# Splitting the packed weights p'·w_in into float32r halves once a batch, straight from PSUM, in an attention-and-FFN kernel

## The chip, the core and the metric

The kernel runs on one core of a Trainium2 chip. A core has a matrix engine (TensorE, PE in the profile; its weight loads are PEld), a vector engine (VectorE, DVE), an activation engine (ScalarE, ACT), GpSimd (POOL), and SyncE (SP), whose queue issues the DMAs here. The metric is the device time of one execution in microseconds (us). Each engine works through its own queue of instructions in order and waits at the head of the queue for what an instruction needs.

## The reference

For 8 batches, 8 heads, 576 tokens and 64 numbers a head, 32 packed queries p first attend to k and v, and then every token's q attends to that packed result, which serves as key and value. The result, 4608 tokens of 512 numbers, passes a two-layer network with a leaky rectifier whose slope alpha is a number per hidden unit.

```python
def sm_attn(qq, kk, vv):
    s = scale * np.matmul(qq, kk.transpose(0, 1, 3, 2))
    s = s - np.max(s, axis=-1, keepdims=True)
    a = np.exp(s)
    a = a / (np.sum(a, axis=-1, keepdims=True) + 1e-09)
    return np.matmul(a, vv)
p_packed = sm_attn(p, k, v)
out = sm_attn(q, p_packed, p_packed)        # (8, 8, 576, 64)
x = out.transpose(0, 2, 1, 3).reshape(B * S, H * D)
h = x @ w_in                                # (4608, 2048)
g = np.maximum(h, 0.0) + alpha * np.minimum(h, 0.0)
return g @ w_out                            # (4608, 512)
```

## The kernel before, in words

Since the second attention multiplies weights a' (32 per head and token) by the packed result p', x·w_in equals a'·(p'·w_in). The kernel therefore never forms x. `attention(b)` makes p' (`p2[b]`) and then the normalised weights a' of a batch (`result[b]`). `packed_w(b, j)` makes p'·w_in for 512 hidden units at a time (j = 0 to 3) with 16 small matmuls (L343) into two PSUM banks, which ScalarE copies to SBUF (L348) as the tile `pw[b, j]`.

The network runs in steps. A step is a pair (k, f): token half k (288 tokens; batch k // 2) and a block f of 128 hidden units. `first(k, f)` multiplies pw by a' into a bank `ps_h` (two of them in turn); ScalarE makes the negated relu (`neg`, L398), VectorE applies alpha in place (L399), ScalarE rounds to float32r (`gh`, L405), and VectorE makes the rest (`gl`, L406). `second(k, f)`, two steps behind, adds gh·w_out high, gh·w_out low and gl·w_out high into four banks `acc` (L416 to L418). Such sums of three products with split operands stand for a float32 product.

For `first` there are two ways. Batches below `XF` = 2 multiply in plain float32: a' is one tile `a_f`, pw is float32, and a step has two matmuls (L384). Later batches split both: a' into `a_h` and `a_l`, made once a batch by ScalarE (L333) and GpSimd (L334), and pw into `pwh` and `pwl` by `split_pw` (L372 and L373 on VectorE), once for each token half and each pair of blocks f, 16 times a batch. A step then has six matmuls (L392 to L394). For batches from 2 on, two instructions of the second softmax (L309, L317) run on GpSimd, for batches 0 and 1 on VectorE.

Batch 0's attention runs alone at the start. After it, 256 steps run. The first 64 cover batches 0 and 1 in four sweeps, so that w_out can arrive in parts: k = 0 and 1 with f = 0 to 3 and then 4 to 7, k = 2 and 3 with f = 0 to 7 (steps 16 to 31), and then all four with f = 8 to 15 (batch 1 in steps 48 to 63). From step 64 on each batch takes 32 steps. In the first 64 steps the weights are also turned from float64 into float32 by ScalarE and VectorE (L101 to L137), after the table `pieces`.

Other work is spread over the steps by tables of step numbers: `attention(b)` is a generator, one stage a step, from step T + 2 with T = 32(b − 1), and `packed_w_steps(b)` reloads w_in from DRAM and calls `packed_w`, at T + 21, 23, 25, 27, 29. What such a step adds is issued behind that step's `first`, relu and alpha (`marks`). Within these bounds a scheduler sets the order of each engine's queue, so a change of one part can reorder the rest.

Of the kernel before, what the change touches and what calls it, by code (L numbers as in the profile page):

```python
# [25 lines left out]
def pack_attention_ffn_kernel(  # L26
# [38 lines left out]
    pwp = ctx.enter_context(tc.tile_pool(name="pwp", bufs=8))  # L65
    pwj = ctx.enter_context(tc.tile_pool(name="pwj", bufs=2))
# [151 lines left out]
    def attention(b):  # L218
# [120 lines left out]
    def packed_w(b, j):  # L339
# [6 lines left out]
        pw[b, j] = pwp.tile([P, 2, 512], F32, name="pw", tag="pw")  # L346
        for r in range(2):
            nc.scalar.copy(out=pw[b, j][:, r, :], in_=banks[r])  # L348
# [19 lines left out]
    def split_pw(k, h):  # L368
        src = pw[k // 2, h // 2][:, :, (h % 2) * 256 : (h % 2) * 256 + 256]
        th = pwj.tile([P, 2, 256], F32R, name="pwh", tag="pwh")  # L370
        tl = pwj.tile([P, 2, 256], F32R, name="pwl", tag="pwl")
        nc.vector.tensor_copy(out=th, in_=src)  # L372
        nc.vector.tensor_tensor(out=tl, in0=src, in1=fv(th), op=ALU.subtract)  # L373
        pj[k, h] = (th, tl)

    def first(k, f):
# [3 lines left out]
        if b < XF:  # L380
            th, a_f = pw[b, f // 4], result[b]
            fs = slice((f % 4) * P, (f % 4) * P + P)
            for i in range(2):
                mm = nc.tensor.matmul(x, th[:, i, fs], a_f[:, i, tok], start=(i == 0), stop=(i == 1))  # L384
        else:
            if (k, f // 2) not in pj:
                split_pw(k, f // 2)
            th, tl = pj[k, f // 2]
# [1 line left out]
            fs = slice((f % 2) * P, (f % 2) * P + P)  # L390
            for i in range(2):
                nc.tensor.matmul(x, th[:, i, fs], a_h[:, i, tok], start=(i == 0), stop=False)  # L392
                nc.tensor.matmul(x, th[:, i, fs], a_l[:, i, tok], start=False, stop=False)  # L393
                mm = nc.tensor.matmul(x, tl[:, i, fs], a_h[:, i, tok], start=False, stop=(i == 1))  # L394
# [142 lines left out]
```

## Time and profile before

| | |
|---|---|
| median of 3 runs | 764.77 us (764.04 to 765.14) |
| profiled execution | 764.46 us |
| its span, first to last instruction | 762.7 us |
| granted TensorE clock, mean | 0.986 |
| TensorE busy | 731.1 us (96%) |
| VectorE busy | 493.5 us (65%) |
| ScalarE busy | 344.9 us (45%) |
| GpSimd busy | 53.1 us (7%) |

A row of a group of instructions reads: line, engine, operation, what it writes `<-` what it reads, shape, count, then busy time and mean ns of one, then idle time of the engine ahead of them and who ended it. A row of the timeline reads: start, length (both us), engine, line, operation, and in brackets the idle time ahead of it with its releaser. Durations of neighbouring instructions of an engine overlap, so what one costs its engine is read from start to start. A float32 matmul of the program appears as more than one MATMUL in the profile. In a row of windows the length is followed by the busy time of PE, PEld, DVE, ACT and POOL, the granted clock, the DMA share and the GB/s.

### The profile page before, as it was taken

The numbers are of one execution on the slowest core, as the hardware profiler recorded it, in microseconds if no ns is written. First come the engines' busy times: TensorE is split into PE (matmuls) and PEld (weight loads), VectorE is DVE, ScalarE is ACT, GpSimd is POOL, SyncE is SP. The second block draws the span as 40 slices with busy tenths as digits, with TensorE's granted clock in tenths as the row PEclk, the third lists the DMA queues.
The fourth block names the chain that finished last, engine by engine and source line by source line (L and its number), as shares of the span: only waits on it lengthen the run. The fifth ranks groups of instructions, "written<-read, shape, count | busy, mean of one in ns | idle before, by whom it ended". The sixth has DMA issues, their size and how long they took to land.

```text
span 762.7 us, 15606 instructions
## 1 busy us (share of the span) xinstructions
PE 731.1 (96%) x6232; PEld 648.2 (85%) x6232; DVE 493.5 (65%) x1019; ACT 344.9 (45%) x795; POOL 53.1 (7%) x74
## 2 busy tenths in 40 slices
PE   4499999999999999999999999999999999999997
PEld 2277788788878999899989999799988999899997
DVE  4887898775545576565855667555765657556663
ACT  4466466663333434443444534444434534443332
POOL 0000000002100021000300012000210003000000
PEclk8699999999999999999999999999999999999999
DMA  8969144044262241422233231422324100200000
GB/s 295 384 226 348 63 166 166 1 137 141 87 197 87 67 126 71 182 86 75 94 113 111 97 119 39 166 88 87 111 78 166 63 2 32 111 33 1 32 1 32
DMA packets 51673, 85.44 MB, mean 112 GB/s; under 512 B 4496, under 2 KB 32144, under 8 KB 51600
## 3 DMA queue, kind: packets, MB, share of 16 engines
q1 hardware_dynamic: 51600, 84.44, 32.1%
q8 instruction: 49, 0.80, 0.4%
q14 instruction: 24, 0.20, 0.1%
HBM read 70.79 MB, written 13.63 MB: 111 GB/s over the span
## 4 chain that ended last, share of the span: by engine, by line
PE 87%; DVE 4%; DMA 4%; ACT 2%; issue 1%; SPq 1%; ACTq 0%; POOL 0%; DVEq 0%
PE acc L416 17%; PE acc L418 17%; PE acc L417 17%; PE ps_h L384 7%; PE ps_h L392 7%; PE ps_h L394 7%; PE ps_h L393 6%; PE ps_m L343 4%; PE ps_m L204 2%; DMA vraw<-in_v 1%; PE ps_m L281 1%; DMA wraw<-in_w_out 1%; PE ps_m L262 1%; DMA wraw<-in_w_in 1%; SPq L121 1%
## 5 line engine op out<-in xcount | busy, mean ns | idle before, releaser
L416 PE MATMUL acc<-gh,wo 128*128 128x288 f32 x1024 | 294.8, 302 | 5.7 <-ACT gh L405 4.5
L417 PE MATMUL acc<-gh,wo 128*128 128x288 f32 x1024 | 290.5, 296 | 0.7 <-DVE wo L137 0.7
L418 PE MATMUL acc<-gl,wo 128*128 128x288 f32 x1024 | 249.7, 306 | 0.0
L416 PEld LDWEIGHTS acc<-gh,wo 128*128 128x128 f32 x1024 | 191.6, 188 | 23.7 <-issue 12.2
L398 ACT ACTIVATE neg<-ps_h 128x288 f32<-128x288 f32 x256 | 105.6, 412 | 208.2 <-PE ps_h L394 155.8
L417 PEld LDWEIGHTS acc<-gh,wo 128*128 128x128 f32 x1024 | 192.5, 188 | 4.1 <-issue 1.7
L399 DVE SCALAR_TENSOR_TENSOR ps_h<-neg,nal,ps_h 128x288 f32<-128x288 f32 x256 | 131.7, 517 | 97.2 <-ACT neg L398 96.8
L418 PEld LDWEIGHTS acc<-gl,wo 128*128 128x128 f32 x1024 | 172.7, 188 | 22.8 <-issue 18.3
L405 ACT CAST gh<-ps_h 128x288 fp32r<-128x288 f32 x256 | 102.4, 400 | 151.2 <-DVE ps_h L399 147.5
L406 DVE TENSOR_TENSOR gl<-ps_h,gh 128x288 fp32r<-128x288 f32 x256 | 115.8, 453 | 77.7 <-ACT gh L405 77.1
L392 PE MATMUL ps_h<-a_h,pwh 128*128 128x288 f32 x384 | 114.6, 298 | 0.0
L394 PE MATMUL ps_h<-a_h,pwl 128*128 128x288 f32 x384 | 114.2, 297 | 0.0
L393 PE MATMUL ps_h<-a_l,pwh 128*128 128x288 f32 x384 | 113.1, 295 | 0.0
L384 PE MATMUL ps_h<-a_f,pw 128*128 128x288 f32 x256 | 75.6, 421 | 8.8 <-DVE z L314 6.7
L392 PEld LDWEIGHTS ps_h<-a_h,pwh 128*128 128x128 f32 x384 | 72.1, 188 | 2.8 <-DVE gl L406 2.3
L394 PEld LDWEIGHTS ps_h<-a_h,pwl 128*128 128x128 f32 x384 | 72.0, 188 | 2.8 <-issue 2.3
L393 PEld LDWEIGHTS ps_h<-a_l,pwh 128*128 128x128 f32 x384 | 72.1, 188 | 0.0
L373 DVE TENSOR_TENSOR pwl<-pw,pwh 128x512 fp32r<-128x512 f32 x96 | 66.8, 697 | 6.5
L372 DVE CAST pwh<-pw 128x512 fp32r<-128x512 f32 x96 | 40.6, 424 | 40.7 <-PE ps_h L393 40.1
L384 PEld LDWEIGHTS ps_h<-a_f,pw 128*128 128x128 f32 x256 | 46.3, 195 | 20.9 <-issue 9.1
L343 PE MATMUL ps_m<-w,p 64*32 64x512 f32 x512 | 38.7, 612 | 0.0
L348 ACT COPY pw<-ps_m 128x512 f32<-128x512 f32 x64 | 34.8, 596 | 2.4 <-PE ps_m L343 2.3
(73 smaller groups left out, 444.5 us busy)
## 6 DMA issues: line engine op xcount, KB each, us to landing
w<-w_whole SPq DMA_DIRECT2D x48, 512.0 KB, 4.0
outT<-ot SPq DMA_DIRECT2D x64, 144.0 KB, 1.9
wraw<-in_w_in SPq DMA_DIRECT2D x8, 1024.0 KB, 11.7
wraw<-in_w_out SPq DMA_DIRECT2D x8, 1024.0 KB, 6.3
xraw<-in_kT SPq DMA_DIRECT2D x28, 288.0 KB, 4.3
xraw<-in_qT SPq DMA_DIRECT2D x28, 288.0 KB, 3.6
vraw<-in_v SPq DMA_DIRECT2D x28, 256.0 KB, 3.5
w_whole<-w SPq DMA_DIRECT2D x8, 512.0 KB, 4.8
```

Source lines behind the costliest of these rows:

```text
L343: nc.tensor.matmul(banks[r][cs, :], p2[b][rs, cs], wi_t[j, pr][rs, :], start=True, stop=True)
L384: mm = nc.tensor.matmul(x, th[:, i, fs], a_f[:, i, tok], start=(i == 0), stop=(i == 1))
L392: nc.tensor.matmul(x, th[:, i, fs], a_h[:, i, tok], start=(i == 0), stop=False)
L393: nc.tensor.matmul(x, th[:, i, fs], a_l[:, i, tok], start=False, stop=False)
L394: mm = nc.tensor.matmul(x, tl[:, i, fs], a_h[:, i, tok], start=False, stop=(i == 1))
L398: nc.scalar.activation(out=neg, in_=x, func=AF.Relu, scale=-1.0),
L399: nc.vector.scalar_tensor_tensor(out=x, in0=neg, scalar=nal[:, f : f + 1], in1=x, op0=ALU.mult, op1=ALU.add),
L405: nc.scalar.copy(out=gh, in_=x)
L406: nc.vector.tensor_tensor(out=gl, in0=x, in1=fv(gh), op=ALU.subtract)
L416: nc.tensor.matmul(ps, wo_t[f][:, 0, os_], gh, start=begin, stop=False)
L417: nc.tensor.matmul(ps, wo_t[f][:, 1, os_], gh, start=False, stop=False)
L418: nc.tensor.matmul(ps, wo_t[f][:, 0, os_], gl, start=False, stop=end)
```

## The change

`XF` becomes 1, so that batch 1 takes the split products too; the constant `EARLY` = 2 keeps what `XF` set for the order of batch 1's loads. `split_pw` goes. For batches from `XF` on `packed_w` writes a tile of both halves: ScalarE's copy out of PSUM rounds to float32r (line 353 of the changed kernel), and VectorE subtracts that from the same PSUM bank (line 354). These tiles are twice as large, and their pool has five buffers in place of eight, with the pool of `split_pw` gone. The second softmax's two instructions run on GpSimd from batch 1 on. Attention starts a step later, and `packed_w` comes at T + 20, 23, 26, 29, with its first reload at T + 17. In the changed kernel L398, L399, L405, L406 are L392, L393, L399, L400, L416 to L418 are L410 to L412, and the split products are L386 to L388.

```diff
-    pwp = ctx.enter_context(tc.tile_pool(name="pwp", bufs=8))
-    pwj = ctx.enter_context(tc.tile_pool(name="pwj", bufs=2))
+    pwp = ctx.enter_context(tc.tile_pool(name="pwp", bufs=5))
...
-        if b < XF:
+        if b < EARLY:
             vs = load_v(b, ("wo2", "wo3") if b == 0 else None)
...
-            eng = nc.vector if b < 2 else nc.gpsimd
+            eng = nc.vector if b < 1 else nc.gpsimd
...
-        pw[b, j] = pwp.tile([P, 2, 512], F32, name="pw", tag="pw")
-        for r in range(2):
-            nc.scalar.copy(out=pw[b, j][:, r, :], in_=banks[r])
+        if b < XF:
+            pw[b, j] = pwp.tile([P, 2, 512], F32, name="pw", tag="pw")
+            for r in range(2):
+                nc.scalar.copy(out=pw[b, j][:, r, :], in_=banks[r])
+        else:
+            pw[b, j] = pwp.tile([P, 2, 2, 512], F32R, name="pw", tag="pw")
+            for r in range(2):
+                hi, lo = pw[b, j][:, 0, r, :], pw[b, j][:, 1, r, :]
+                nc.scalar.copy(out=hi, in_=banks[r])
+                nc.vector.tensor_tensor(out=lo, in0=banks[r], in1=fv(hi), op=ALU.subtract)
...
-    def split_pw(k, h):
-        src = pw[k // 2, h // 2][:, :, (h % 2) * 256 : (h % 2) * 256 + 256]
-        th = pwj.tile([P, 2, 256], F32R, name="pwh", tag="pwh")
-        tl = pwj.tile([P, 2, 256], F32R, name="pwl", tag="pwl")
-        nc.vector.tensor_copy(out=th, in_=src)
-        nc.vector.tensor_tensor(out=tl, in0=src, in1=fv(th), op=ALU.subtract)
-        pj[k, h] = (th, tl)
...
+        w, fs = pw[b, f // 4], slice((f % 4) * P, (f % 4) * P + P)
+        for i in range(2):
+            if b < XF:
+                mm = nc.tensor.matmul(
+                    x, w[:, i, fs], result[b][:, i, tok], start=(i == 0), stop=(i == 1)
+                )
+                continue
             a_h, a_l = result[b]
...
+            nc.tensor.matmul(x, w[:, 0, i, fs], a_h[:, i, tok], start=(i == 0), stop=False)
+            nc.tensor.matmul(x, w[:, 0, i, fs], a_l[:, i, tok], start=False, stop=False)
+            mm = nc.tensor.matmul(x, w[:, 1, i, fs], a_h[:, i, tok], start=False, stop=(i == 1))
...
-    XF = 2
+    EARLY, XF = 2, 1
...
-    add(a1, [2 + n * 4 // 5 for n in range(15)])
+    add(a1, [3 + n * 4 // 5 for n in range(15)])
     for b in range(2, B):
         T = 32 * (b - 1)
-        add(attention(b), range(T + 2, T + 2 + 18))
-        add(packed_w_steps(b), [T + 21 + 2 * n for n in range(NJ + 1)])
+        add(attention(b), range(T + 3, T + 3 + 18))
+        add(packed_w_steps(b), [T + n for n in (17, 20, 23, 26, 29)])
```

How the queues are ordered at the three places that the prediction speaks of follows. The first is VectorE's queue at the end of batch 1's attention, about steps 13 to 15 (t_707 and t_742 are the two token halves before, t_726 and t_761 now; z is the sum and its reciprocal, s the transposed half). Before:

```order
L313 TENSOR_REDUCE z_891<-t_742 128x18
L315 RECIPROCAL z_819<-z_819 128x18
L399 SCALAR_TENSOR_TENSOR ps_h<-neg,nal,ps_h 128x288
L314 TENSOR_SCALAR z_891<-z_891 128x18
L317 TENSOR_TENSOR t_707<-t_707,z_819 128x576
L399 SCALAR_TENSOR_TENSOR ps_h<-neg,nal,ps_h 128x288
L315 RECIPROCAL z_891<-z_891 128x18
L406 TENSOR_TENSOR gl<-ps_h,gh 128x288
L327 STREAM_TRANSPOSE a_f<-t_707 128x2x288
L317 TENSOR_TENSOR t_742<-t_742,z_891 128x576
```

The same place now:

```order
L314 RECIPROCAL z_842<-z_842 128x18
L354 TENSOR_TENSOR pw<-ps_m,pw 128x512
L312 TENSOR_REDUCE z_916<-t_761 128x18
L354 TENSOR_TENSOR pw<-ps_m,pw 128x512
L393 SCALAR_TENSOR_TENSOR ps_h<-neg,nal,ps_h 128x288
L331 STREAM_TRANSPOSE s_849<-t_726 128x576
L313 TENSOR_SCALAR z_916<-z_916 128x18
L400 TENSOR_TENSOR gl<-ps_h,gh 128x288
L314 RECIPROCAL z_916<-z_916 128x18
L393 SCALAR_TENSOR_TENSOR ps_h<-neg,nal,ps_h 128x288
L331 STREAM_TRANSPOSE s_947<-t_761 128x576
L354 TENSOR_TENSOR pw<-ps_m,pw 128x512
```

The multiplications by z have left this queue, and the subtractions of p'·w_in stand in it. On GpSimd's queue, where batch 1 had nothing, there now stand, in this order:

```order
L308 TENSOR_TENSOR t_726<-t_726,m_812 128x576
L308 TENSOR_TENSOR t_761<-t_761,m_890 128x576
L316 TENSOR_TENSOR t_726<-t_726,z_842 128x576
L316 TENSOR_TENSOR t_761<-t_761,z_916 128x576
L333 TENSOR_TENSOR a_l<-s_849,a_h 128x2x288
L333 TENSOR_TENSOR a_l<-s_947,a_h 128x2x288
```

So the first half's a_l is behind the second half's multiplication. The second place is TensorE's queue at the first step of batch 1, step 16 (wo_815 before and wo_809 now are the w_out blocks of the steps 14 and 15). Before:

```order
L418 MATMUL acc_947<-gl,wo_815 128x288
L416 MATMUL acc_948<-gh,wo_815 128x288
L384 MATMUL ps_h<-a_f,pw 128x288 x2
L417 MATMUL acc_948<-gh,wo_815 128x288
L418 MATMUL acc_948<-gl,wo_815 128x288
```

Now, with 13 matmuls of `second` left out where the dots are:

```order
L410 MATMUL acc_952<-gh,wo_809 128x288
L386 MATMUL ps_h<-a_h,pw 128x288
L412 MATMUL acc_951<-gl,wo_809 128x288
...
L411 MATMUL acc_953<-gh,wo_809 128x288
L387 MATMUL ps_h<-a_l,pw 128x288
L388 MATMUL ps_h<-a_h,pw 128x288
L386 MATMUL ps_h<-a_h,pw 128x288
```

The first product with a_h stands seven matmuls of `second` earlier than the float32 product did, and the first one with a_l comes 15 matmuls of `second` behind it. The third place is VectorE's queue where k turns from 4 to 5 (steps 80 and 81), the two `ot` being copies of the finished `acc`. Before:

```order
L406 TENSOR_TENSOR gl<-ps_h,gh 128x288
L372 CAST pwh<-pw 128x512
L313 TENSOR_REDUCE z_3197<-t_3023 128x18
L433 COPY ot<-acc_2625 128x288
L433 COPY ot<-acc_2627 128x288
L373 TENSOR_TENSOR pwl<-pw,pwh 128x512
L399 SCALAR_TENSOR_TENSOR ps_h<-neg,nal,ps_h 128x288
```

Now:

```order
L393 SCALAR_TENSOR_TENSOR ps_h<-neg,nal,ps_h 128x288
L306 TENSOR_REDUCE m_3305<-t_3173 128x18
L331 STREAM_TRANSPOSE s_3275<-t_3134 128x576
L400 TENSOR_TENSOR gl<-ps_h,gh 128x288
L427 COPY ot<-acc_2755 128x288
L427 COPY ot<-acc_2757 128x288
L393 SCALAR_TENSOR_TENSOR ps_h<-neg,nal,ps_h 128x288
```

The pair that splits pw is gone from between the copies of `acc` and the next alpha step, and the softmax of that batch stands a step or more further back (its reduction L306, L307 before, was behind step 79 and is behind step 80).

More of the change, by code (lines that the diff above doesn't have):

```diff
@@ L81, in pack_attention_ffn_kernel @@
     nal = const.tile([P, NF], F32, name="nal")
-    wo_t, wi_t, p2, result, pw, pj, gs, part, acc, marks = {}, {}, {}, {}, {}, {}, {}, {}, [], []
+    wo_t, wi_t, p2, result, pw, gs, part, acc, marks = {}, {}, {}, {}, {}, {}, {}, [], []
     def drain(gen):
@@ L238, in attention @@
         yield
-        if b >= XF:
+        if b >= EARLY:
             vs = load_v(b)
@@ L270, in attention @@
             yield
-        if b >= XF:
+        if b >= EARLY:
             qs = load_x(qT, b)
@@ L379, in first @@
         x = ps[:, :HS]
[L380 to L388, printed above, removed]
-            a_h, a_l = result[b]
[L390 to L394, printed above, removed]
+        w, fs = pw[b, f // 4], slice((f % 4) * P, (f % 4) * P + P)
[5 more added lines that the diff above has]
+                continue
+            a_h, a_l = result[b]
+            nc.tensor.matmul(x, w[:, 0, i, fs], a_h[:, i, tok], start=(i == 0), stop=False)
+            nc.tensor.matmul(x, w[:, 0, i, fs], a_l[:, i, tok], start=False, stop=False)
+            mm = nc.tensor.matmul(x, w[:, 1, i, fs], a_h[:, i, tok], start=False, stop=(i == 1))
         neg = gp.tile([P, HS], F32, name="neg", tag="neg", bufs=2)
```

## The prediction

> **What bounds the kernel now.** I read the page first: the span and the busy shares, then the end chain by engine.
>
> ```profile
> span 762.7 us, 15606 instructions
> PE 731.1 (96%) x6232; PEld 648.2 (85%) x6232; DVE 493.5 (65%) x1019; ACT 344.9 (45%) x795; POOL 53.1 (7%) x74
> PE 87%; DVE 4%; DMA 4%; ACT 2%; issue 1%; SPq 1%; ACTq 0%; POOL 0%; DVEq 0%
> ```
>
> TensorE is busy 96% of the span and carries 87% of the chain; VectorE, which does the splitting that the change reduces, carries 4%. So VectorE's time is worth nothing by itself; only what TensorE does, or waits for, counts. An average hides stages, so I cut the span into windows at steps 0, 16, 32, 48, 64 (a step is one `first` and one `second`) and at batch borders; columns are length, then busy time of PE, PEld, DVE, ACT, POOL.
>
> ```profile
> 37.60:96.40 58.80, 55.38 (x459) 42.70 (x459) 48.99 (x91) 35.40 (x73) 0.73 (x4) 0.97 0.58 209
> 96.40:143.00 46.60, 45.52 (x293) 38.69 (x293) 39.63 (x66) 27.90 (x52) 0.00 (x0) 1.00 0.36 136
> 143.00:194.40 51.40, 50.77 (x444) 41.41 (x443) 34.35 (x71) 27.75 (x64) 6.76 (x9) 1.00 0.39 119
> 194.40:242.30 47.90, 47.90 (x329) 38.61 (x328) 20.69 (x47) 17.10 (x40) 1.43 (x1) 1.00 0.35 118
> 330.90:419.20 88.30, 88.00 (x797) 80.75 (x796) 55.79 (x123) 38.50 (x95) 8.60 (x10) 1.00 0.31 103
> ```
>
> From step 16 on TensorE is dense: 1.08 us idle in 96 to 143, 0.63 in the next window, none in the next, 0.3 in each 88.3 us batch. Only before step 16 is 3.4 us idle. Two things can pay: fewer TensorE cycles in batch 1, whose steps are 16 to 31 and 48 to 63, and the few waits that VectorE causes.
>
> **The change part by part.** *Batch 1's product a'·(p'w_in).* It goes from 2 matmuls in full float32 to 6 in float32r. A dense step of each kind, by its first matmul and the next step's:
>
> ```profile
> 231.64 1.13 PE L384 MATMUL ps_h<-a_f,pw 128*128 128x288 f32 x4
> 232.40 0.51 PE L416 MATMUL acc<-gh,wo 128*128 128x288 f32 x1
> 234.19 1.13 PE L384 MATMUL ps_h<-a_f,pw 128*128 128x288 f32 x4
> 402.86 0.31 PE L392 MATMUL ps_h<-a_h,pwh 128*128 128x288 f32 x1
> 403.67 0.30 PE L416 MATMUL acc<-gh,wo 128*128 128x288 f32 x1
> 405.26 0.30 PE L392 MATMUL ps_h<-a_h,pwh 128*128 128x288 f32 x1
> ```
>
> The two float32 matmuls appear as four passes. The float32 step takes 234.19 − 231.64 = 2.55 us, the split step 405.26 − 402.86 = 2.40. Six products (0.81, to 403.67) are cheaper than four passes with their tail. Batch 1 has 32 steps: 32 × 0.15 = **4.8 us less** on the engine that bounds.
>
> *The split of p'w_in.* Gone are 16 pairs of L372 and L373 for each of batches 2 to 7; in come 8 subtractions from PSUM (line 354 of the changed kernel) for each of batches 1 to 7. ScalarE's copy (L348) only changes its output type.
>
> ```profile
> L372 DVE CAST pwh<-pw 128x512 fp32r<-128x512 f32 x96 | 40.6, 424 | 40.7 <-PE ps_h L393 40.1 <-ACT pw L348 0.5
> L373 DVE TENSOR_TENSOR pwl<-pw,pwh 128x512 fp32r<-128x512 f32 x96 | 66.8, 697 | 6.5
> L406 DVE TENSOR_TENSOR gl<-ps_h,gh 128x288 fp32r<-128x288 f32 x256 | 115.8, 453 | 77.7 <-ACT gh L405 77.1
> L348 ACT COPY pw<-ps_m 128x512 f32<-128x512 f32 x64 | 34.8, 596 | 2.4 <-PE ps_m L343 2.3
> ```
>
> No 128x512 subtraction from PSUM stands here. L406 is one of 288 columns from PSUM (453 ns), L373 one of 512 from SBUF (697): 0.45 is the lower end, 453 × 512/288 = 0.81 the upper. I take 0.70, as L373 has the same size. VectorE loses 107.4 us and gains 56 × 0.70 = 39: 68 us less, all of it beside TensorE. What reaches TensorE is one wait a batch, where token half k turns from even to odd:
>
> ```profile
> 285.92 0.43 DVE L372 CAST pwh<-pw 128x512 fp32r<-128x512 f32 x1 [0.30 <-PE ps_h L393]
> 286.26 0.75 DVE L313 TENSOR_REDUCE z<-t 128x18 f32<-128x576 f32 x1
> 286.92 0.81 DVE L433 COPY ot<-acc 128x288 f32<-128x288 f32 x2
> 287.65 0.68 DVE L373 TENSOR_TENSOR pwl<-pw,pwh 128x512 fp32r<-128x512 f32 x1
> 288.25 0.51 DVE L399 SCALAR_TENSOR_TENSOR ps_h<-neg,nal,ps_h 128x288 f32<-128x288 f32 x1
> 288.64 0.29 PE L418 MATMUL acc<-gl,wo 128*128 128x288 f32 x1
> 289.25 0.40 PE L416 MATMUL acc<-gh,wo 128*128 128x288 f32 x1 [0.32 <-ACT gh L405]
> PE acc L416 <- ACT gh L405: 1.5, 5, 0.3
> ```
>
> L416 begins 0.61 us after L418 where products stand 0.81/6 = 0.13 apart: 0.48 lost, because L399 stood behind the pair L372/L373 (1.0 us by starts). The last row, waits after 245 us, counts five. With the pair gone L399 comes before the copies of `acc`: **5 × 0.48 = 2.4 us less**. The new subtractions stand at steps T+20, 23, 26, 29, behind that step's L406, and are done (596 ns cast, 2 × 0.70: 2.0 us) before the next step, 2.4 us later, needs the queue. Lower bound of this term 0 (another instruction takes the place), upper 2.4; I take 2.3.
>
> *Batch 1's attention on GpSimd.* Four VectorE instructions (L309 and L317, 0.74 each) go to GpSimd, and two low-part subtractions (L334) and two casts come in. Everything now passes one queue, which the order of the change gives as two L309, two L317, two L334, so the first a_l waits for the second half's L317.
>
> ```profile
> L309 POOL TENSOR_TENSOR t<-t,m 128x576 f32<-128x576 f32 x12 | 14.4, 1200 | 111.3 <-DVE m L307 111.3
> L334 POOL TENSOR_TENSOR a_l<-s,a_h 128x576 fp32r<-128x576 f32 x12 | 19.1, 1594 | 20.1 <-ACT a_h L333 20.1
> L317 POOL TENSOR_TENSOR t<-t,z 128x576 f32<-128x576 f32 x12 | 13.9, 1161 | 42.8 <-DVE z L315 42.8
> 87.13 0.26 DVE L315 RECIPROCAL z<-z 128x18 f32<-128x18 f32 x1
> 89.30 0.77 DVE L327 STREAM_TRANSPOSE a_f<-t 128x576 f32<-128x576 f32 x1
> 92.39 1.13 PE L384 MATMUL ps_h<-a_f,pw 128*128 128x288 f32 x4
> 97.54 0.40 PE L416 MATMUL acc<-gh,wo 128*128 128x288 f32 x1 [0.30 <-DVE part L429]
> ```
>
> Before, a_f was there at 90.07 and wanted at 92.39. Now: half 0's reciprocal ends at 85.9 (two L309 earlier) to 87.4; then by VectorE's order two subtractions, one L313 and one L399, 2.65 us, and the transpose, 0.77; half 1's reciprocal behind one L406, 0.7, at 90.0 to 91.5; L317 1.16, L334 1.59: a_l at 92.8 to 94.3. TensorE wants it after 15 `second` matmuls that now stand behind the first product, which itself stands 7 matmuls earlier: 92.39 − 0.93 + 0.13 + 15 × 0.13 = 93.5. Stall 0 to 0.8 us; I take 0.4. VectorE's sum before step 16 stays equal: 4 × 0.74 out, 4 × 0.70 in. The wait for `part` at 97.54 stays.
>
> *Start order.* Attention 1 begins a step later and steps 2 to 15 are queued anew. In that stage TensorE idles 3.4 us; a gain of 1.5 or a loss of 1.5 are the bounds, zero is taken. Shorter steps in 16 to 31, where VectorE is busy 39.6 of 46.6 us, leave less room before each use: up to the whole 2.4 us of that half may go back to waits for L399. I take 0.2, as the waits there now are 1.1 us in all.
>
> *Nothing.* The loads one step later, and the reloads of w_in at T+17 (two of 512 KB on SP's queue, four times a batch, ahead of or among the four output stores), are wanted three steps later, 7 us:
>
> ```profile
> w<-w_whole SPq DMA_DIRECT2D x48, 512.0 KB, 4.0
> ```
>
> If a reload took 4 us more, TensorE would wait 1 us at that `packed_w`. Five pw buffers hold: the copy at step T+20+3j takes the one last read at step T+15+4j, two steps free at the tightest (j = 3).
>
> *Sum*, against the profiled 764.46 us (span 762.7, 1.8 around it): −4.8 − 2.3 + 0.4 + 0.2 = −6.5, so 757.96; the runs' median 764.77 stands 0.3 higher: **758.2 us**. Its own range, from both ends of the terms (−8.7 to −1.5 − 2.4 = −3.9): 756 to 761.
>
> **A rule that speaks against the change.** The trace's GpSimd rows spread: L334 averages 1594 ns, L317 1161, while VectorE works beside them. The Trainium skill, "SBUF — State Buffer", section "SBUF: two separate sides", says that GpSimd and VectorE share a port pair as an exclusive lock: a VectorE instruction in a two-port mode, or with two SBUF inputs, and a GpSimd one keep each other out for their whole length. By that rule the five GpSimd instructions up to a_l could each lose one 1.22 us conversion step, 6.1 us in all, and the sum would be near 763; the rows of L317 agree with no loss at all, those of L334 with a third of it.
>
> **The rivals.** *GpSimd's chain is late and the start's pace eats the gain.* For it: VectorE is busy 49.0 of 58.8 us before step 16, where GpSimd so far had only 0.73 us of work. If each of five instructions loses what L334's mean has over L317's, 0.43, a_l comes 2.2 us later, a stall of up to 3.0; with the 2.4 us of steps 16 to 31 lost too, 758.2 + 2.6 + 2.2 = 763. Middle: 761. Against it: GpSimd rows in 143 to 194, VectorE busy 67%, show no such loss in L317.
>
> *The change doesn't do what it says:* the six products cost what the four passes did, since pw's halves now lie further apart and weights load slower, and only the waits go: 758.2 + 4.8 = 763.0. Against it, the weights of the split product (256 columns a tile) and of batch 0's (512) load alike, beside the products:
>
> ```profile
> L392 PEld LDWEIGHTS ps_h<-a_h,pwh 128*128 128x128 f32 x384 | 72.1, 188 | 2.8 <-DVE gl L406 2.3
> L384 PEld LDWEIGHTS ps_h<-a_f,pw 128*128 128x128 f32 x256 | 46.3, 195 | 20.9 <-issue 9.1 <-DVE gl L406 3.4 <-DVE mag L103 0.5
> ```
>
> *Slower: VectorE's queue stands at its head.* One mechanism: each new subtraction waits in order for ScalarE's cast, and the transposes of s2 for GpSimd; L399 and L406 behind them come late. A packed step holds the queue 0.60 + 2 × 0.70 = 2.0 us. It decides once more than 1.5 us of that falls after the next `first` has ended; if half of the 28 packed steps lose 0.6 us, that is 8.4: 758.2 + 8.4 = 766.6. Against it: in the order the pair stands behind L406, and the next relu is a step, 2.4 us, away.
>
> **How the numbers follow.** Forecast 0.57, the late chain 0.22, no cheaper product 0.09, slower 0.12. About 0.2%, 1.5 us, is what a measurement of this kernel can tell from no change. Faster (under 763.2): 0.55 + 0.17 + 0.05 = 0.77; same 0.12, slower 0.11. The range leaves out the slower case and a little below: 755 to 763.
>
> **What would show it.** Right: L386 to L388 six apart by 0.13 us in steps 16 to 31 and 48 to 63, with steps near 2.40; stage 194 to 242 shorter by 2.4 us; batches of 87.8 us instead of 88.3; no wait of L410 for ScalarE's gh at odd k; the last L333 of half 0 in batch 1 ended by 94. Wrong: waits of the a_l product for GpSimd over 1 us, the wait at odd k still there under another instruction, or new waits of TensorE for L393 behind line 354.

## The result, and the profile after

The changed kernel took **753.36 us** (median of 4 runs, 752.91 to 755.82), the kernel before 764.41 us beside it (4 runs, 764.04 to 765.14): a ratio of **0.9856**, 95% interval 0.9844 to 0.9869. It is faster by 11.0 us; the forecast was 758.2, faster by 6.5, in a range of 755 to 763. In two later measurements the same kernel gave 754.59 and 754.91 us, ratios 0.9866 (0.9853 to 0.9880) and 0.9878 (0.9865 to 0.9892). So the gain is 9.7 to 11.0 us: the sign was right, the size was a third or more too small, and the time lies 1.6 us below the range.

The page of the changed kernel, its span, busy shares and end chain (its profiled execution took 755.82 us, the slowest of the four):

```profile
span 754.0 us, 15743 instructions
PE 723.7 (96%) x6296; PEld 650.6 (86%) x6296; DVE 435.1 (58%) x879; ACT 344.1 (46%) x797; POOL 59.1 (8%) x80
PE 91%; ACT 3%; DVE 2%; DMA 1%; issue 1%; SPq 0%; POOL 0%; ACTq 0%; POOLq 0%
```

TensorE still bounds: it is busy for the same share and carries more of the chain. VectorE lost 58 us of work (493.5 to 435.1), TensorE 7.4 (731.1 to 723.7). The windows of the changed kernel, cut at the same steps (0, 16, 32, 48, 64, and the batch from step 96):

```profile
38.30:98.10 59.80, 56.54 (x464) 43.86 (x464) 50.13 (x94) 36.80 (x75) 9.02 (x10) 0.95 0.56 208
98.10:142.90 44.80, 42.80 (x320) 39.29 (x321) 38.56 (x63) 27.50 (x51) 0.00 (x0) 1.00 0.42 142
142.90:193.10 50.20, 49.56 (x443) 41.20 (x441) 34.35 (x69) 26.84 (x62) 2.95 (x6) 1.00 0.30 101
193.10:237.20 44.10, 44.10 (x365) 39.46 (x362) 26.66 (x56) 17.93 (x41) 5.14 (x4) 1.00 0.46 153
324.70:412.30 87.60, 87.60 (x797) 80.58 (x796) 45.67 (x99) 38.17 (x95) 8.14 (x10) 1.00 0.31 104
```

Steps 48 to 63 went from 47.9 to 44.1 us, a batch from 88.3 to 87.6 with no idle time of TensorE left in it. The stages (us), with two profiled executions of the changed kernel (the second is from the repetition below), since they differ before step 16:

| | steps 0–3 | 4–15 | 16–31 | 32–47 | 48–63 | 64–223 (five batches) | 224–255 |
|---|---|---|---|---|---|---|---|
| before, 764.46 | 15.55 | 43.28 | 46.55 | 51.45 | 47.85 | 441.58 | 74.10 |
| changed, 755.82 | 15.86 | 43.95 | 44.84 | 50.19 | 44.06 | 438.01 | 74.11 |
| changed, 753.17 | 13.74 | 43.45 | 44.85 | 50.21 | 44.06 | 438.01 | 74.11 |
| changed less before | −1.8 to +0.3 | +0.2 to +0.7 | −1.7 | −1.2 | **−3.8** | **−3.6** | 0 |

The last column ends with TensorE's last matmul. The part before step 0's `second` took 37.6 us before and 38.3 now. From step 16 on the two executions of the changed kernel agree to 0.02 us. The 2 us in steps 0 to 3 between them are the clock, which is shown at the end, and no part of the change; the 0.5 us in steps 4 to 15 were not followed up.

### The profile page after: what moved, and what is told of

It reads as the page before. It is cut to its first block, busy times and chain, and to the rows that moved or that the text cites. A ratio compares the mean times of both kernels' runs of the same rounds, so it can differ in the third digit from the quotient of the medians.

```text
span 754.0 us, 15743 instructions
## 1 busy us (share of the span) xinstructions
PE 723.7 (96%) x6296; PEld 650.6 (86%) x6296; DVE 435.1 (58%) x879; ACT 344.1 (46%) x797; POOL 59.1 (8%) x80
## 4 chain that ended last, share of the span: by engine, by line
PE 91%; ACT 3%; DVE 2%; DMA 1%; issue 1%; SPq 0%; POOL 0%; ACTq 0%; POOLq 0%
PE acc L412 18%; PE acc L410 18%; PE acc L411 18%; PE ps_h L386 8%; PE ps_h L388 8%; PE ps_h L387 8%; PE ps_m L342 4%; PE ps_h L381 4%; PE ps_m L203 2%; PE ps_m L280 2%; PE ps_m L261 1%; DMA wraw<-in_w_in 1%; ACT low L101 1%; ACT w L100 1%; ACT mag L100 0%
## 5 line engine op out<-in xcount | busy, mean ns | idle before, releaser
L410 PE MATMUL acc<-gh,wo 128*128 128x288 f32 x1024 | 293.5, 300 | 7.1 <-ACT gh L399 5.5
L412 PE MATMUL acc<-gl,wo 128*128 128x288 f32 x1024 | 251.1, 303 | 0.0
L393 DVE SCALAR_TENSOR_TENSOR ps_h<-neg,nal,ps_h 128x288 f32<-128x288 f32 x256 | 133.1, 520 | 185.6 <-ACT neg L392 184.6
L392 ACT ACTIVATE neg<-ps_h 128x288 f32<-128x288 f32 x256 | 105.4, 412 | 225.5 <-PE ps_h L388 204.0
L410 PEld LDWEIGHTS acc<-gh,wo 128*128 128x128 f32 x1024 | 192.4, 189 | 14.7 <-ACT gh L399 8.3
L412 PEld LDWEIGHTS acc<-gl,wo 128*128 128x128 f32 x1024 | 173.3, 189 | 29.7 <-issue 27.8
L400 DVE TENSOR_TENSOR gl<-ps_h,gh 128x288 fp32r<-128x288 f32 x256 | 116.3, 455 | 85.6 <-ACT gh L399 83.8
L399 ACT CAST gh<-ps_h 128x288 fp32r<-128x288 f32 x256 | 102.2, 399 | 126.8 <-DVE ps_h L393 125.6
L386 PE MATMUL ps_h<-a_h,pw 128*128 128x288 f32 x448 | 133.7, 298 | 0.1
L388 PE MATMUL ps_h<-a_h,pw 128*128 128x288 f32 x448 | 132.5, 296 | 0.0
L387 PE MATMUL ps_h<-a_l,pw 128*128 128x288 f32 x448 | 132.0, 295 | 0.0
L386 PEld LDWEIGHTS ps_h<-a_h,pw 128*128 128x128 f32 x448 | 84.1, 188 | 6.2 <-DVE gl L400 3.0
L388 PEld LDWEIGHTS ps_h<-a_h,pw 128*128 128x128 f32 x448 | 84.1, 188 | 0.0
L387 PEld LDWEIGHTS ps_h<-a_l,pw 128*128 128x128 f32 x448 | 84.1, 188 | 0.0
L381 PE MATMUL ps_h<-a_f,pw 128*128 128x288 f32 x128 | 40.7, 440 | 6.5 <-DVE z L313 6.4
L381 PEld LDWEIGHTS ps_h<-a_f,pw 128*128 128x128 f32 x128 | 23.6, 202 | 15.9 <-issue 9.1
L354 DVE TENSOR_TENSOR pw<-ps_m,pw 128x512 fp32r<-128x512 f32 x56 | 36.2, 683 | 1.3 <-ACT pw L353 0.5
L342 PE MATMUL ps_m<-w,p 64*32 64x512 f32 x512 | 36.8, 615 | 0.0
L182 POOL MEMSET vraw<- 64x128 f32 x28 | 4.6, 198 | 398.9 <-PE ps_m L280 398.7
L353 ACT CAST pw<-ps_m 128x512 fp32r<-128x512 f32 x56 | 30.5, 597 | 1.1 <-PE ps_m L342 1.0
```

The source lines that it names most:

```text
L342: nc.tensor.matmul(banks[r][cs, :], p2[b][rs, cs], wi_t[j, pr][rs, :], start=True, stop=True)
L381: mm = nc.tensor.matmul(x, w[:, i, fs], result[b][:, i, tok], start=(i == 0), stop=(i == 1))
L386: nc.tensor.matmul(x, w[:, 0, i, fs], a_h[:, i, tok], start=(i == 0), stop=False)
L387: nc.tensor.matmul(x, w[:, 0, i, fs], a_l[:, i, tok], start=False, stop=False)
L388: mm = nc.tensor.matmul(x, w[:, 1, i, fs], a_h[:, i, tok], start=False, stop=(i == 1))
L392: nc.scalar.activation(out=neg, in_=x, func=AF.Relu, scale=-1.0),
```

## The experiments

Twelve kernels ran, in three groups of four, each group on one chip with the kernel before beside it (764.25, 764.75 and 764.64 us). The change has four parts that can be taken alone: the **split** from PSUM once a batch, the split **product** for batch 1, the **tables** of steps, and batch 1's softmax on **GpSimd**. In the diffs a minus line is the kernel that is named, a plus line the experiment.

### The change again, and the change without one part

The changed kernel, unaltered:

> The changed kernel once more, unaltered, for a second profile: the profiled execution of the first was 755.82 us, 2.5 us over the median of its runs, and the extra time can only lie where its trace shows the lower granted clock (0.98 against 0.986), in the first 40 us. Theory A (the 11.0 us are 4.8 of cheaper products, 3.6 of batches 2 to 6 and the rest from the first 64 steps): 753.4 us, batches at 87.6 us each, and steps 0 to 15 shorter than 59.8 us by about 2.4. Theory B (the first profile's steps 0 to 15 are typical and the other runs are short elsewhere): batches below 87.3 us, steps 0 to 15 at 59.8.

754.59 us (753.17 to 754.71, 4 runs), ratio 0.9866 (0.9853 to 0.9880). Theory A by its stages: batches of 87.6 us, and steps 0 to 15 in 57.2 instead of 59.8.

Batch 1 back to the float32 product, all else as changed:

```diff
-    EARLY, XF = 2, 1
+    EARLY, XF = 2, 2
```

> The changed kernel with batch 1's product back in plain float32 (XF = 2), all else as changed: the split once a batch from PSUM for batches 2 to 7, GpSimd, step tables. Theory A (the product is worth what two dense steps show, 32 x 0.15 us): 753.4 + 4.8 = 758.2 us, with steps 16 to 31 and 48 to 63 each 2.4 longer and the batches from step 64 unchanged at 87.6. Theory B (the product is worth more than dense steps show, since the order around it pays too): 760.5 to 762. Theory C (the start is paced by VectorE, the product worth little): under 756.

757.61 us (756.84 to 758.28, 4 runs), ratio 0.9907 (0.9892 to 0.9922): 3.0 us slower than the changed kernel, close to theory A. (Batch 1's pw and a' stay whole then, so 8 subtractions on VectorE and two on GpSimd go with the product.) By stages (profiled executions of both) the product is worth 3.00 us in steps 16 to 31 (47.85 against 44.85), 0.61 in 32 to 47 and 1.46 in 48 to 63, 5.1 in all, but steps 4 to 15 are 1.1 us longer with it (43.45 against 42.34). Two things are new in this stage: one `packed_w` of batch 1 is cut in two on TensorE's queue, which is priced below, and a wait stands at its end. The timeline of the changed kernel there:

```profile
95.29 1.14 ACT L100 ACTIVATE w<-wraw 128x1024 f32<-128x1024 f32 x1
95.43 0.52 DVE L393 SCALAR_TENSOR_TENSOR ps_h<-neg,nal,ps_h 128x288 f32<-128x288 f32 x1 [1.37 <-ACT neg L392]
96.32 1.13 ACT L101 ACTIVATE low<-wraw 128x1024 uint32<-128x1024 uint32 x1
97.34 0.41 ACT L392 ACTIVATE neg<-ps_h 128x288 f32<-128x288 f32 x1
97.63 0.40 ACT L399 CAST gh<-ps_h 128x288 fp32r<-128x288 f32 x1
98.09 0.40 PE L410 MATMUL acc<-gh,wo 128*128 128x288 f32 x1 [1.61 <-ACT gh L399]
```

VectorE's alpha (L393) ends at 95.95, but ScalarE's gh starts only at 97.63: two instructions of a w_in conversion, of 1.14 and 1.13 us, and a further relu stand between on its queue. TensorE idles 1.61 us.

The old step tables, all else as changed:

```diff
-    add(a1, [3 + n * 4 // 5 for n in range(15)])
+    add(a1, [2 + n * 4 // 5 for n in range(15)])
...
-        add(attention(b), range(T + 3, T + 3 + 18))
-        add(packed_w_steps(b), [T + n for n in (17, 20, 23, 26, 29)])
+        add(attention(b), range(T + 2, T + 2 + 18))
+        add(packed_w_steps(b), [T + 21 + 2 * n for n in range(NJ + 1)])
```

> The changed kernel with the step tables of before (attention from T+2, attention 1 from step 2, packed_w at T+21, 23, 25, 27, 29). Theory A (the tables are worth little, the splitting itself frees VectorE): 753.4 to 754.4 us, batches at 87.6. Theory B (the tables carry the part of the gain that the prediction lacked, 4 us, by keeping the pieces of p'w_in whole on TensorE and the softmax away from the turn of k): 756.5 to 757.5, batches at 88.0 or more.

758.66 us (758.26 to 760.24, 5 runs), ratio 0.9928 (0.9915 to 0.9940), above both forecasts: the tables, which the prediction put at zero, are worth 4.1 us on top of the rest. By stages 1.66 us of it lie in steps 48 to 63 (45.72 against 44.06), 0.97 in 32 to 47, 0.70 in 4 to 15, 0.6 in the five batches; steps 16 to 31 are 0.4 shorter with the old tables.

### One part alone

The split product for batch 1 in the kernel before, by the old `split_pw`:

```diff
-    XF = 2
+    EARLY, XF = 2, 1
```

(with `EARLY` in place of `XF` in the three tests that order the loads)

> The kernel before with batch 1's product split and nothing else: split_pw serves batch 1 too (16 more pairs of L372 and L373, 17.9 us of VectorE in the first 64 steps), a_h and a_l are made for batch 1 with its two softmax instructions still on VectorE. Theory A (TensorE is the bound even there): 764.4 - 4.8 = 759.6 us, batches from step 64 unchanged at 88.2. Theory B (VectorE paces steps 16 to 31, where it is busy 39.6 of 46.6 us, and 9 us more fall there): the gain of that half is lost, 762 to 764.

764.86 us (764.49 to 766.85, 11 runs), ratio 1.0009 (0.9999 to 1.0019): no gain, a little above theory B. The tables alone, the same edit as above the other way round in the kernel before:

> The kernel before with nothing changed but the three step tables (attention of batch 1 and of batches 2 to 7 a step later, `packed_w` three steps apart); products and the old split pair stay as they were. Putting the tables back in the changed kernel cost 4.1 to 5.2 us, 1.7 of it in steps 48 to 63, where TensorE's small matmuls of `packed_w` then stand in more pieces. Theory A (the tables pay by themselves, through fewer switches between small and large matmuls: 12 pieces of `packed_w` instead of 15 before step 62, and none of it depends on VectorE): 764.3 - 4 = about 760, stage 48 to 63 at 46.2 or less instead of 47.85, batches unchanged at 88.3. Theory B (the tables pay only with the short split: as long as the pair of 1.1 us per two steps stands on VectorE's queue, what the pieces give back is lost to waits for gh): 763 to 766, stage 48 to 63 shorter but batches longer, or steps 0 to 31 longer.

764.93 us (763.41 to 766.85, 11 runs), ratio 1.0002 (0.9991 to 1.0013): no gain, as theory B has it. The split from PSUM alone, in the kernel before, for batches 2 to 7 (the change's lines of `packed_w`, `first` and the pools, with the old tables):

```diff
-    XF = 2
+    EARLY, XF = 2, 2
```

> The kernel before with the split of p'w_in made straight from PSUM, once a batch (five buffers), for batches 2 to 7; batch 1 keeps the product in float32, the old step tables stay. Theory A (the wait for gh at odd k goes with the pair, and a little of the waits inside a batch): five batches of 87.7 instead of 88.3, in all 3 us less, 761; steps 0 to 47 unchanged. Theory B (the subtractions, with old tables two steps apart, make waits of their own as large as those that go): 764, batches at 88.2 or more. Theory C (the rest of the change's gain hangs on the split too, since VectorE is relieved of 60 us): below 759.

760.57 us (759.62 to 761.40, 5 runs), ratio 0.9945 (0.9933 to 0.9957): 4.2 us faster, as theory A has it. Product and tables together, with the old split:

> The kernel before with both the split product for batch 1 and the new step tables, but still with the old split pair (128x512 cast and subtraction from SBUF every second step, now for batch 1 too). The product alone gave 0, the tables alone 0, the new split alone 4.2 us, all together 10. Theory B (product and tables pay only where VectorE has no long pair on its queue): no gain from the two together either, 763 to 767, the batches at 89.0 as with the tables alone. Theory A (the parts add up, and the two zeros were losses that each makes in steps 4 to 31 and that the other takes away): 758 to 761.

764.98 us (763.01 to 766.26, 12 runs), ratio 1.0004 (0.9995 to 1.0013): no gain either; by the time theory B stands. Together with the runs above this fills a square, as the difference to the kernel before beside each:

| | neither | product | tables | both |
|---|---|---|---|---|
| old split | 0 | +0.6 | +0.2 | +0.3 |
| split from PSUM | **−4.2** | **−5.6** | **−6.6** | **−9.7** |

The lower row's last three have batch 1's softmax on GpSimd besides. With it back on VectorE, both together gave −9.6 (under "Batch 1's softmax on VectorE" below), so the four corners can be compared; the two single cells of the lower row have no such run. Product and tables are worth nothing under the old split and 5.5 us under the new one. So the effects of the parts taken singly don't add up to that of the change. By stages most of this difference lies in the five batches: with product and tables they grow by 3.9 us under the old split (445.5 against 441.6) and shrink by 0.6 under the new one (438.0 against 438.7).

Where the gain goes under the old split is read from the traces. First, the tables alone. TensorE's waits after step 64, from the trace of that kernel, and its batch from step 96 as a window, below it the same window with the split alone:

```profile
PE ps_h L392 <- DVE gl L406: 1.7, 5, 0.3
PE acc L416 <- DVE ot L433: 1.3, 5, 0.3
328.74:417.76 89.02, 88.42 (x797) 80.71 (x796) 57.84 (x123) 37.98 (x95) 8.25 (x10) 1.00 0.32 102
```

```profile
328.27:416.04 87.77, 87.77 (x797) 80.75 (x796) 45.71 (x99) 38.25 (x95) 8.15 (x10) 1.00 0.31 104
```

With the old split the later attention meets the pair L372/L373, on VectorE's queue and on GpSimd beside it. From the timeline of the tables alone, at the first such place:

```profile
278.36 1.34 POOL L317 TENSOR_TENSOR t<-t,z 128x576 f32<-128x576 f32 x1 [2.16 <-DVE z L315]
278.78 1.46 DVE L373 TENSOR_TENSOR pwl<-pw,pwh 128x512 fp32r<-128x512 f32 x1
280.17 0.51 DVE L399 SCALAR_TENSOR_TENSOR ps_h<-neg,nal,ps_h 128x288 f32<-128x288 f32 x1
282.83 0.40 PE L392 MATMUL ps_h<-a_h,pwh 128*128 128x288 f32 x1 [0.35 <-DVE gl L406]
283.81 1.16 DVE L372 CAST pwh<-pw 128x512 fp32r<-128x512 f32 x1 [0.66 <-PE ps_h L393]
```

L373 takes 1.46 us, where its median over this run is 0.69: it ends 0.54 us after GpSimd's L317, which had begun before it. The alpha step behind it (L399) starts at 280.17, though its relu was done at 278.85. L372 is stretched too, from 0.43 to 1.16, beside GpSimd's L309 (283.52 to 284.68), and TensorE's second wait, at 285.47, stands behind it. Every one of the five batches has one L373 of 1.46 and two L372 of 0.90 to 1.23. That is 2.0 us a batch more on VectorE, which the windows show: 57.84 us busy with 123 instructions, against 55.79 with as many in the kernel before, where no L372 is above 0.43 and no L373 above 0.86. In the changed kernel the subtraction from PSUM (L354) never takes more than 0.69, beside GpSimd's instructions too. No run takes the stretching away and leaves the rest, so what it costs apart from the order of the queue is not shown.

So TensorE waits twice a batch for VectorE, 1.7 + 1.3 = 3.0 us in all, where the kernel before waits once, for gh, 1.5 in all. Of the 3.7 us by which the five batches grow (445.25 against 441.58) the waits show 1.5; the rest is no idle time in the profile and was not followed up. Under the new split the same tables make no wait, and the batches shrink by 0.6. Steps 48 to 63 gain 2.3 us from the tables alone (47.85 to 45.51), and steps 4 to 15 gain 1.6 (43.28 to 41.64); the batches eat 3.7 of that, and steps 16 to 31 lose 2.0 (48.57 against 46.55), 1.3 of it in a wait for gh at 121.71 behind a w_in conversion.

Second, the product alone. Its gain of 1.7 us in steps 48 to 63 and 0.4 in 32 to 47 is taken back in steps 4 to 15 (45.58 against 43.28). A row and a window of its timeline at step 16:

```profile
99.03 0.40 PE L416 MATMUL acc<-gh,wo 128*128 128x288 f32 x1 [2.53 <-ACT gh L405]
100.00:104.00 4.00, 4.00 (x20) 3.98 (x19) 3.84 (x6) 2.34 (x4) 0.00 (x0) 0.57 0.33 100
```

It is the wait behind the w_in conversion again, 2.53 us here, and behind it the granted clock stands at 0.57 for a window of 4 us. Steps 16 to 31 then take 47.20 us, longer than before, though TensorE's work in them is the cheaper one. This loss does not need the pair: the changed kernel with batch 1's softmax on VectorE has the same wait and the same clock behind it (below). Why the two together gain nothing under the old split shows in the same two places, a wait of 2.55 us at step 16 and the longer batches.

### Which table, and what it does

The changed kernel with only `packed_w`'s times put back:

```diff
-        add(packed_w_steps(b), [T + n for n in (17, 20, 23, 26, 29)])
+        add(packed_w_steps(b), [T + 21 + 2 * n for n in range(NJ + 1)])
```

> The changed kernel with one of its three step tables put back: `packed_w` of batches 2 to 7 again at T+21 to T+29 two steps apart, reads of w_in one step apart from it; attention stays a step later. Theory A (this table carries the 4 to 5 us: by the order of TensorE's instructions `packed_w` again stands in 15 pieces, not 13, before step 62, and the steady batches lose 0.17 each): 757.5 to 759.5, stage 48 to 63 at 45.7 instead of 44.1. Theory C (the later start of the attentions carries it): 753.5 to 755, stage 48 to 63 near 44.1.

755.84 us (755.27 to 758.54, 5 runs), ratio 0.9892 (0.9876 to 0.9909), between the two forecasts. By stages this table alone makes 2.28 us in steps 48 to 63 (46.34 against 44.06), 0.2 in the five batches (438.20 against 438.01) and at most 0.04 in each stage before. The 2.28 us lie in how often TensorE turns from the large matmuls to the small ones of `packed_w`. The 16 small matmuls of one `packed_w`, as the profile counts them, in the kernel before, after the row of their group a whole one, then one that the scheduler has cut in three:

```profile
L343 PE MATMUL ps_m<-w,p 64*32 64x512 f32 x512 | 38.7, 612 | 0.0
208.63 1.09 PE L343 MATMUL ps_m<-w,p 64*32 64x512 f32 x16
209.65 0.80 PE L418 MATMUL acc<-gl,wo 128*128 128x288 f32 x4
...
218.66 1.06 PE L343 MATMUL ps_m<-w,p 64*32 64x512 f32 x8
219.66 0.40 PE L416 MATMUL acc<-gh,wo 128*128 128x288 f32 x1
...
220.16 0.29 PE L416 MATMUL acc<-gh,wo 128*128 128x288 f32 x1
220.38 1.04 PE L343 MATMUL ps_m<-w,p 64*32 64x512 f32 x2
221.36 0.40 PE L416 MATMUL acc<-gh,wo 128*128 128x288 f32 x1
...
222.53 0.29 PE L418 MATMUL acc<-gl,wo 128*128 128x288 f32 x1
222.75 1.06 PE L343 MATMUL ps_m<-w,p 64*32 64x512 f32 x6
223.73 0.40 PE L417 MATMUL acc<-gh,wo 128*128 128x288 f32 x1
```

And the third `packed_w` of this stage in the changed kernel:

```profile
215.71 1.09 PE L342 MATMUL ps_m<-w,p 64*32 64x512 f32 x16
216.73 0.40 PE L410 MATMUL acc<-gh,wo 128*128 128x288 f32 x1
```

A whole one holds TensorE for 209.65 − 208.63 = 1.02 us. The pieces of 8, 2 and 6 hold it for 1.00, 0.98 and 0.98: a piece of two costs what 16 cost. The reason stands in the rows' own times. One takes 0.61 us, and yet 16 are over in 1.09, so they run side by side. In the trace of the whole one eight start within 0.05 us, the other eight from 0.45 us on, and the next large matmul 0.52 behind the last of these. The program has eight small matmuls here, one a head, each of them two rows (not 16 matmuls, as the description of the kernel has it: 256 in the whole run appear as 512). A piece of two rows is one head, and one head alone takes as long as eight together. A cut makes heads run one after the other.

From the start of the large matmul ahead of them (220.16 and 222.53) the last two pieces take 1.20 each, of which 0.13 would pass between large matmuls anyway: 1.00 + 1.20 + 1.20 − 2 × 0.13 = 3.1 us, **2.1 us more** for the same work. In the changed kernel every `packed_w` of this stage is whole. The other runs agree, in steps 48 to 63: the split alone leaves two pieces (2 and 14 rows) instead of three and takes 1.15 us less than the kernel before, the tables alone leave it whole and take 2.34 less. None of this shows as idle time, since the modelled ends of the small matmuls reach over it (1.04 us for two). The Trainium skill, "TensorEngine Tiling (Array Packing)", section "Tiling Modes", says in its key properties that a change of the tiling mode drains TensorE; no run here parts such a drain from the rest of a turn. By the trace it can be only a small part: a small matmul starts 0.22 us behind the large one ahead of it and the second large one 0.24 behind the first, where large ones follow each other by 0.13, an estimate of 0.2 to 0.3 us a turn, where a head alone holds TensorE for 0.98.

### Batch 1's softmax on VectorE

```diff
-            eng = nc.vector if b < 1 else nc.gpsimd
+            eng = nc.vector if b < 2 else nc.gpsimd
```

> The changed kernel with the four subtractions and multiplications of batch 1's softmax back on VectorE; only the two subtractions for a_l stay on GpSimd. On GpSimd they cost TensorE nothing that the trace shows (a_l is there 1.35 us before it is wanted), and they free VectorE of 4 x 0.74 us in steps 4 to 16. Theory A (in steps 4 to 16 VectorE's queue decides, so 3 us more on it cost 0.5 to 2 us there): 755 to 756.5, stage 4 to 16 above 43.9. Rival (that stage is decided by the loads and by ScalarE, and the move to GpSimd was worth nothing): 753.5 to 754.8, stage 4 to 16 at 43.0 to 43.6.

755.00 us (752.97 to 756.15, 4 runs), ratio 0.9873 (0.9857 to 0.9890), beside 754.91 of the changed kernel on that chip: no difference that four runs each can show. The two forecasts are not told apart: the time is theory A's, while steps 4 to 15 take 43.28 us, as the rival has it. But steps 16 to 31 take 46.72, 1.9 more than in the changed kernel. The wait at step 16 and the window around it, from this kernel's timeline and windows:

```profile
94.76 0.61 PE L410 MATMUL acc<-gh,wo 128*128 128x288 f32 x1 [2.54 <-ACT gh L399]
94.00:98.00 4.00, 3.24 (x15) 3.24 (x16) 3.96 (x6) 1.11 (x4) 0.00 (x0) 0.57 0.20 14
```

It waits 2.54 us instead of 1.6, and the clock behind it is at 0.57, as with the product alone. In this execution 0.7 us of the 1.9 are given back in steps 4 to 15 (44.00 in the changed kernel on that chip), where no `packed_w` is cut as one is in the changed kernel, and 1.0 in steps 0 to 3, by the clock. Whether other executions have the lower clock at step 16 too isn't shown, so what the move to GpSimd is worth stays open between nothing and 1.2 us.

### A conversion two steps later

```diff
-    pieces = {... 15: "1", 16: "I", 18: "Io", 20: "Oo", ...}
+    pieces = {... 15: "1", 18: "I", 19: "Io", 20: "Oo", ...}
```

> The changed kernel with the conversion of w_in that stands at step 16 moved to step 18, and the one at 18 to 19. In the changed kernel TensorE waits 1.61 us at 95.4 us for gh, which stands behind that conversion's two instructions (1.13 and 1.12 us) on ScalarE. Theory A (ScalarE's order makes that wait): it goes, steps 0 to 31 are 1.0 to 1.8 us shorter, 752 to 753.3. Rival (the conversion is only late work that has to be done somewhere: it now delays another gh or the `packed_w` that needs it): no difference, 754 to 755.

753.55 us (751.28 to 754.15, 5 runs), ratio 0.9847 (0.9831 to 0.9864), a little above theory A's range. Since the changed kernel itself was not in that group, both ran once more on one chip:

> The kernel with the conversion of w_in two steps later once more, beside the changed kernel on the same chip. Its trace had stage 4 to 16 shorter by 0.98 us and stage 16 to 32 longer by 0.14, all other stages equal to 0.01 us. Theory A: 0.5 to 1.2 us below the changed kernel here. Rival: no difference that the runs can tell, within 0.3 us.

> The changed kernel unaltered, as the one to compare with on this chip: 753.4 to 754.6, stages 64 to 224 at 87.5 to 87.7 each.

753.26 us (752.82 to 754.47, 4 runs) with the later conversion, 754.91 (754.67 to 756.11, 4 runs) without; the ranges don't meet. (The first measurement of the changed kernel, 753.36, does lie among the times of the later conversion, so the stages below are the better evidence.) TensorE's waits for gh over the whole span, of the changed kernel and then with the later conversion:

```profile
PE acc L410 <- ACT gh L399: 6.0, 5, 2.4
```

```profile
PE acc L410 <- ACT gh L399: 3.2, 5, 1.9
96.27 0.40 PE L410 MATMUL acc<-gh,wo 128*128 128x288 f32 x1 [0.26 <-DVE part L423]
```

The wait of 1.6 us at step 16 is gone, and what is left there is 0.26 us for `part`. Stage 4 to 15 is 1.0 to 1.6 us shorter (42.47 and 42.39 against 43.45 and 44.00), stage 16 to 31 0.1 longer, and all later stages up to step 223 equal to 0.03 us. So the wait was ScalarE's order and not its load, and this version beats both kernels: 11.2 and 11.4 us under the kernel before.

## Why the prediction fell short, by its own steps

**What bounds, and the signs: right.** TensorE is as dense as before, all the gain is in its work and its waits, and the 58 us taken from VectorE pay only through TensorE's waits. (The prediction's 68 us are a sum of rows, and the rows of the two traces differ by 70; the busy time of the page counts overlaps once.) But that last point has a side that the prediction missed: a sum of terms supposes that the parts don't meet, and under the old split the tables met the pair L372/L373 beside GpSimd, which took their gain back.

**Batch 1's product, −4.8: right in size, lost in part.** A product's six matmuls in steps 48 to 63 of the changed kernel stand 0.13 us apart and take 0.79 (predicted 0.81):

```profile
203.97 0.30 PE L386 MATMUL ps_h<-a_h,pw 128*128 128x288 f32 x1
...
204.76 0.30 PE L410 MATMUL acc<-gh,wo 128*128 128x288 f32 x1
```

In steps 16 to 63 it is worth 5.1 us. At step 16 it brings the wait of 1.6 us that the prediction did not have ("the wait for `part` at 97.54 stays" named another one). The rival that the product is not cheaper falls.

**The split's waits, −2.3: too small.** The new subtraction takes what was taken for it, and no wait at odd k is left: the first gh matmul follows the last of the half before by 0.14 us, before the copies of `acc` even begin. From the groups and the timeline of the changed kernel:

```profile
L354 DVE TENSOR_TENSOR pw<-ps_m,pw 128x512 fp32r<-128x512 f32 x56 | 36.2, 683 | 1.3 <-ACT pw L353 0.5
279.79 0.43 PE L412 MATMUL acc<-gl,wo 128*128 128x288 f32 x2
280.06 0.30 PE L410 MATMUL acc<-gh,wo 128*128 128x288 f32 x1
280.13 0.99 DVE L427 COPY ot<-acc 128x288 f32<-128x288 f32 x2 [0.37 <-PE acc L412]
```

683 ns stand against the 0.70 us taken. With the split alone the five batches shrink by 0.90, 0.54, 0.48, 0.48 and 0.54, 2.9 us against the upper bound of 2.4: 0.48 in each, as worked out, and 0.4 more in the first, which was not followed up. The split also took 1.15 us from steps 48 to 63 (47.85 to 46.70), where `packed_w` is cut once less; the prediction had no term for that. Its cover for the subtractions held. This is the whole list of TensorE's waits from 143 to 700 us in the changed kernel, and it names neither L393 nor gh:

```profile
PE acc L410 <- ACT part L425: 0.6, 1, 0.6
```

**GpSimd's chain, +0.4: nothing.** The view of the tile a_l in the changed kernel lists its subtractions, and under those who waited for it nobody:

```profile
L333 POOL TENSOR_TENSOR a_l<-s,a_h x14: 1422/1433/1441, 91.3 to 636.9; 128x576 fp32r<-128x576 f32 x14
91.28 1.44 POOL L333 TENSOR_TENSOR a_l<-s,a_h 128x576 fp32r<-128x576 f32 x1
94.07 0.29 PE L387 MATMUL ps_h<-a_l,pw 128*128 128x288 f32 x1
```

The first half is done at 92.72 and wanted at 94.07. The forecast of 92.8 to 94.3 against 93.5 was a little pessimistic at both ends. The subtraction's 1433 ns hardly vary (1422 to 1441). Before, their mean of 1594 hid two kinds: seven of 1.43 to 1.45 us, and five of 1.80 to 1.81 that each began 0.17 us behind an L373 on VectorE. The rule of the port that the prediction weighed from the Trainium skill, "SBUF — State Buffer", section "SBUF: two separate sides", would have cost each of five instructions up to 1.22 us. One of the five did lose: the first L308 of batch 1 took 2.00 us beside VectorE's L136 (78.75 to 79.96), 0.84 more than the second:

```profile
78.98 2.00 POOL L308 TENSOR_TENSOR t<-t,m 128x576 f32<-128x576 f32 x1 [8.78 <-DVE m L306]
```

L316 took 1.16 us in both places of batch 1 and L333 1.44 and 1.42. The loss did not reach TensorE. So the rule speaks for the change as much as against it: with the tables alone it is the old pair L372/L373 that GpSimd's instructions stretch, and the trace agrees there (L373 1.46 us instead of 0.69), while the subtraction that replaces the pair reads PSUM and is not stretched in any row of the changed kernel.

**The step tables, "start order" and "nothing": this is the step that failed.** The prediction put the tables at zero (bounds of ±1.5 for steps 2 to 15, 0.2 for steps 16 to 31) and looked only for waits and late loads. It counted nothing on TensorE for them; the number of instructions there does not change. What changed was how they are grouped: `packed_w` in 13 runs instead of 15 before step 62, by the order of the instructions on TensorE, and all four of batch 2's whole. That is 2.3 us in steps 48 to 63. A step's later attention also moves eight rows of its score matmuls (L203) over the border at step 48, so that 32 to 47 shows 0.6 to 1.0 us too much gain and 48 to 63 as much too little. With 0.6 in the batches and 0.7 in steps 4 to 15, the tables are, under the new split, 2.4 us without the product and 4.1 with it. Steps 16 to 31, where 0.2 was taken as lost, came out 1.7 us shorter against 2.4 − 0.2 = 2.2 by the terms.

Stage by stage the terms gave −2.2 in 16 to 31, 0 in 32 to 47, −2.4 in 48 to 63, −2.3 in the batches; measured −1.7, −1.2, −3.8, −3.6. The misses in the last three add to 3.9 us, and they are the tables, the split's side effect on the cutting of `packed_w`, and 0.6 us of the product that fell in 32 to 47. The prediction's own range of 756 to 761 had no room for them: all its terms at their best gave −8.7. Its upper end, −3.9, does not follow from its terms, which at their worst give −4.8 + 0 + 0.8 + 1.5 + 2.4 = −0.1.

**The rivals.** GpSimd's late chain, the product that is not cheaper and VectorE's queue standing at its head: none came. The range ended at 755.0 because the bounds of the terms did; the one that was missing, the cutting, could have been read from the three pieces at 218.66 to 223.73 of the kernel before.

## What to carry to other kernels

On an engine that is 96% busy, look at the order of its own instructions for changes of shape, and not only at its waits: one small matmul alone between large ones held TensorE as long as eight that run side by side (0.98 and 1.02 us), and such time counts as busy. Before pricing several edits as a sum, ask which of them the others will run into, and look at the longest row of a group beside its mean: here two edits were worth 0 with the old pair L372/L373 and 5.5 us without it. And a conversion that may run at any time should not be issued where a result is due at the next step; two steps later it cost 0.1 us in its new place and gave 1.0 to 1.6.

## What the runs showed of the hardware that was not expected

**The clock comes back at different times at the start.** In two executions of the same changed kernel the window 40 to 44 us reads, first in the slower one (755.82 us), then in the faster (753.17 us):

```profile
40.00:44.00 4.00, 4.00 (x15) 3.43 (x14) 2.75 (x5) 1.42 (x3) 0.00 (x0) 0.50 0.45 178
```

```profile
40.00:44.00 4.00, 4.00 (x37) 2.94 (x36) 3.27 (x5) 2.16 (x5) 0.00 (x0) 1.00 0.33 130
```

With TensorE busy 4.00 us both times, the one does 15 matmul records at half clock and the other 37 at full. The full clock comes back for good at 44.1 us in the one and at 36.7 in the other. Steps 0 to 3 took 15.86 and 13.74 us, and 14.77 in a third execution (754.67 us): most of what parts the three. A stage table has to leave it out. The Trainium skill, "TensorE: Matmul & The Clock Gate", section "Part 1: The HAM clock gate (the "warmup" mystery)", says that the gate works by free-running windows of 3.4 us and that the slow start therefore varies from run to run; the trace agrees, the effect here being 2.1 us of 754.

**Gaps of 2.5 us were followed by the half clock.** Behind TensorE's waits of 2.53 us (the product alone) and 2.54 us (softmax on VectorE) the granted clock was 0.57 over 4 us, and a stretch of half clock as long (3.4 us) stands behind the 2.55 us of product and tables together; behind waits of 1.61 us (the changed kernel) and 1.87 (with the old tables) it stayed at 1.00. These are five gaps and no threshold. A wait near that length was priced too low by its idle time alone: softmax on VectorE lengthened the wait at step 16 by 0.9 us, and steps 16 to 31 behind it by 1.9.
